# Two mixture layers behind an attention on one core: four accumulator banks by name, twelve first copies on VectorE, a last partial sum scaled early

## The chip, the core and the metric

The kernel runs on one core of a Trainium2 chip. The metric is the time of one execution on the device in microseconds (us). The core has five engines that work beside each other, each in the order of its own instructions: TensorE (PE) for matmuls, VectorE (DVE), ScalarE (ACT), GpSimd (POOL) and SyncE (SP), which here only starts transfers (DMAs). Matmuls write into PSUM, eight banks of 128 x 512 words; all else works out of SBUF. An instruction waits for those of other engines by semaphores.

## The reference

```python
def _attn_ref(q, k, v, w_pre, w_post):          # (4, 12, 448, 64)
    scores = scale * np.matmul(q, k.transpose(0, 1, 3, 2))
    scores = np.einsum('bhij,hg->bgij', scores, w_pre)
    attn = softmax(scores)
    attn = np.einsum('bhij,hg->bgij', attn, w_post)
    return np.matmul(attn, v)

def _moe_ref(x, w_in, w_out):                   # 1792 x 768, 768 x 2048, 2048 x 768
    h = x @ w_in
    g = np.where(h > 0.0, h, np.exp(np.minimum(h, 0.0)) - 1.0)
    return g @ w_out

def _moe2_ref(x, w_in, w_out, g_ln):            # 768 x 1024, 1024 x 768
    h = x @ w_in
    solu = h * softmax(h)
    ln = (solu - mu) / np.sqrt(var + 1e-06) * g_ln
    return ln @ w_out
```

The output of each is the input of the next. The weights of both layers arrive as float64 words.

## The kernel before

Attention fills the time to about 360, the first mixture layer ("first MoE") 360 to 821, the second 822 to the end. Every float32 matmul is made of three, from operands split into a high part and a remainder.

**First MoE.** The 2048 hidden features are cut into eight groups `fg` of 256, the tokens into four blocks `tb` of 448. For each (fg, tb), `hid` (line 377) makes two tiles of 128 features in 18 matmuls each; `elu` turns one into g by ACT (Relu, line 391, and Exp, line 392) and DVE (line 393), and ACT and POOL split g into `gh` and `glo` (lines 388, 389). `outp(fg, tb)` (line 872) makes six tiles `e` of 128 output features, six matmuls each (line 883), and brings every tile out of its PSUM bank into the accumulator `x1[tb]`: in group 0 by an ACT copy (line 897), later by a DVE addition (line 900). PE runs hid of one block, then outp of the block before it. The tiles of `outp` come from a pool `ps_o` of four banks under one tag; the pool decides which of the four is next. When the loop is done the pool's banks go to the second MoE.

**Filler work.** Between these steps stands work that needs no PE. Weights are loaded as 64-bit words into a ring `ws` of four buffers (SP, line 210) and decoded: DVE clamps (line 218), ACT scales (line 219), and DVE shifts, takes the sign and joins (lines 223, 227, 231). Six pieces per group are the next `fg`'s weights. After these, the second MoE's weights are made and stored to DRAM: `wi_spill` (twelve pieces) and `w2_group(k)`, k from 0 to 3. A group decodes four blocks of `w_out`, p12, p11, p22 and p21, takes differences T1, T3, T2, T4 (DVE, line 320) for a multiplication by Strassen's scheme in Winograd's form, and splits and stores seven results (ACT cast, line 333; POOL subtraction, line 334; a DMA from POOL's queue, line 341). p21's load takes the buffer of an earlier store.

The order on each engine is that of the code, and a small planner places the filler: `run` and `work` keep a modelled time of PE and of DVE, `paced(until)` issues filler steps of 0.78 us (`DVE_STEP`) as long as DVE's modelled time stays below `until`, and `tick` takes the next step whose landing time (`land`, `PD`) is over. In the last group, after outp(7, 1) has been written, `drain(True)` issues all filler steps that are left with these landing times ignored.

**Second MoE.** `hid2(t)` (line 1022) makes 14 token tiles of h, each in two PSUM banks; softmax and the normalisation's moments follow. Then seven products per pair of token tiles, P1 to P7 (line 1094), and `behind` (line 1096) adds each one to partial sums in `ob`: c11, c12 of one token tile, c21, c22 of the next. P5's bank is also added to c12 (line 1114); P3, the last product, is added to c12. What is final is multiplied by the normalisation's factor `col(9, t)` on ACT (line 1117) and goes out by DMA.

Of the kernel before, what the change touches and what calls it, by code (L numbers as in the profile page):

```python
# [9 lines left out]
F32 = mybir.dt.float32  # L10
# [3 lines left out]
AF = mybir.ActivationFunctionType  # L14
ALU = mybir.AluOpType
AX = mybir.AxisListType
PSUM = bass.MemoryType.PSUM

NB, NH, S, D = 4, 12, 448, 64
DM, F1, F2 = 768, 2048, 1024  # L20
NT = NB * S
ECH = DM // 128
# [50 lines left out]
def kernel(ctx: ExitStack, tc: tile.TileContext, qa, kt, vt, wpre, wpost,  # L73
# [4 lines left out]
    nc = tc.nc  # L78
# [3 lines left out]
    def pool(name, bufs=1, side="left", space=None):  # L82
        kw = {"space": space} if space is not None else {"side": side}
        p = tc.alloc_tile_pool(name=name, bufs=bufs, reuse_waits="tile", **kw)
        pools[name] = p
        return p
# [56 lines left out]
    pe_t, dve_t = 0.0, 0.0  # L143

    def run(us):

        nonlocal pe_t, dve_t
        dve_t = max(dve_t, pe_t)
        pe_t += us

    def work(us, ready=0.0):

        nonlocal dve_t
        dve_t = max(dve_t, ready) + us
# [86 lines left out]
    def w1_ready(fg, pieces):  # L241

        while fg and any((fg, i) not in w1_done for i in pieces):
            work(DVE_STEP)
            tick(1, force=True)
# [122 lines left out]
    def hid(fg, tb, ft, kcs=range(ECH)):  # L368
        wh, wl = w1[fg][0], w1[fg][1]
        xh, xl = xT[tb]  # L370
        if kcs[0] == 0:
            ring, p = ("sc", ps_sc) if (tb, ft) not in ((1, 1), (3, 1)) else ("h", ps_h)
            h_t[fg, tb, ft] = p.tile([128, 512], F32, tag=ring, name="h")
        ps = h_t[fg, tb, ft]
        for kc in kcs:
            for n, (a, x) in enumerate(((wh, xh), (wh, xl), (wl, xh))):
                nc.tensor.matmul(ps[:, :S], a[:, kc * FG + ft * 128:kc * FG + (ft + 1) * 128], x[:, kc, :],  # L377
                                 start=kc == 0 and n == 0, stop=kc == ECH - 1 and n == 2)
# [32 lines left out]
    def op(rank, emit, deps=(), new=(), uses=(), more=0.0, lag=None, port=False, **us):  # L411

        o = Op()
        o.port = port
        o.rank, o.emit, o.deps, o.new, o.us, o.more, o.lag = rank, emit, [d for d in deps if d is not None], new, us, more, lag
        for b in chain(new, uses):
            b.users.append(o)
        ops.append(o)
        return o
# [73 lines left out]
    t, nf, t_hid = T0, 0, None  # L493
# [36 lines left out]
    def dma(out, in_, e="sp"):  # L530
        {"act": nc.scalar, "pool": nc.gpsimd, "sp": nc.sync}[e].dma_start(out=out, in_=in_)
# [63 lines left out]
    o = op(7.0, lambda e: dma(wpre_t, wpre), sp=.5, lag=7.0)  # L595
# [37 lines left out]
    for u, sl in enumerate(units):  # L633
# [62 lines left out]
        o = op(r0 + 3.2, guard, ex, [], [sb], port=True, dve=.07)  # L696
        o = op(r0 + 3.3, inv, [o], [], [sb], dve=.07)
        ow = op(r0 + 3.4, weigh, [o, o_wpost], [wb], [sb], port=True, dve=.3, pool=.38)
        r0 = t_post[u]
        o = op(r0, post, ex + [ow], pob, eb + [wb], pe=POST)  # L700
# [5 lines left out]
    for c in range(NC):  # L706
# [12 lines left out]
        for n in range(2):  # L719
# [11 lines left out]
            o = op(r, mm, at_ops[c] + ov, [avb], [vb, at_b[c]], pe=AV * w / 120)  # L731
# [10 lines left out]
            o = op(r + AV + .2, take, [o], [xb], [avb], act=.36, dve=.42)  # L742
# [4 lines left out]
    for n in range(16):  # L747
        sl = slice((n % 8) * 192, (n % 8) * 192 + 192)
        src, dst = (wo1 if n > 7 else wi1)[0, :, sl], w1s[n // 8][:, sl]
# [38 lines left out]
        o = op(t0, load, [last], [sb], sp=.5, lag=11.0)  # L788
        o = op(t0 + 4, clamp, [o], [], [sb], dve=.17)
        oa = op(t0 + 4.5, scale, [o], [], [sb], act=.26)  # L790
        o = op(t0 + 5, loword, [o], [], [sb], dve=.17)
        o = op(t0 + 5.5, sign, [o], [], [sb], dve=.27)
        o = op(t0 + 6, join, [oa, o], [], [sb], dve=.27)
# [55 lines left out]
    for ft in range(2):  # L849
        o = None  # L850
        for p in range(3):
            o = op(t_hid + HD + ft * .01, lambda e, ft=ft, p=p: hid(0, 0, ft, range(2 * p, 2 * p + 2)),
                   need + [o] + [sc_ev[lc, h] for h in range(NH)], pe=HID / 3)
# [10 lines left out]
    x1 = [x1_p.tile([128, ECH, S], F32, tag=f"x1_{tb}", name=f"x1_{tb}", bufs=1) for tb in range(NB)]  # L864
# [3 lines left out]
    for tb in range(2, NB):  # L868
        xT_alloc(tb, pool(f"xT{tb}"))
    ps_h = pool("ps_h", 1, space=PSUM)  # L870
    ps_o = pool("ps_o", 4, space=PSUM)
    def outp(fg, tb, rest):
        w1_ready(fg, range(3, 6))
        wh, wl = w1[fg][2], w1[fg][3]
        gs = [g_t.pop((fg, tb, ft)) for ft in range(2)]
        for e in range(ECH):
            run(1.21)
            ps = ps_o.tile([128, 512], F32, tag="o", name="o")
            n = 0
            for ft in range(2):  # L880
                gh, glo = gs[ft]
                for a, x in ((wh, gh), (wl, gh), (wh, glo)):
                    nc.tensor.matmul(ps[:, :S], a[:, ft * DM + e * 128:ft * DM + (e + 1) * 128], x,  # L883
                                     start=n == 0, stop=n == 5)
                    n += 1
            if fg == 0 and tb < 2:
                if e % 2 == 0:
                    x_hi(tb + 2, e // 2)
                else:
                    x_lo(tb + 2, e // 2, nc.vector)  # L890
                    if tb == 0:
                        x_load(3, e // 2)
            else:
                paced(pe_t + DVE_LAG)
            spend(1.13)
            if fg == 0:
                nc.scalar.copy(x1[tb][:, e, :], ps[:, :S])  # L897
            else:
                work(.61, pe_t + .1)
                nc.vector.tensor_tensor(x1[tb][:, e, :], x1[tb][:, e, :], ps[:, :S], ALU.add)  # L900
            if rest:
                if len(rest) == 2:
                    work(.61)
                rest.pop(0)()
# [91 lines left out]
    def col(i, t, n=1):  # L996
        return sm[:, i, t:t + n]
# [98 lines left out]
    def behind(q, x):  # L1096


        t, n = 2 * q, 384
        ps = bank.pop(x)[:, :n]  # L1100
        if x in ("P1", "P7"):
            ob_t[t + (x == "P7")] = pools["wstg"].tile([128, 1024], F32, tag="ws", name="ob", bufs=4)
        c11, c12 = (ob_t[t][:, i * n:i * n + n] for i in range(2))
        if x == "P1":
            nc.scalar.copy(c11, ps)
            return
        if x in ("P6", "P2"):
            dst, src = (c12, c11) if x == "P6" else (c11, c11)
        else:
            c21, c22 = (ob_t[t + 1][:, i * n:i * n + n] for i in range(2))  # L1110
            dst, src = {"P7": (c21, c12), "P5": (c22, c21), "P4": (c21, c21), "P3": (c12, c12)}[x]
        nc.vector.tensor_tensor(dst, ps, src, ALU.add)
        if x == "P5":
            nc.vector.tensor_tensor(c12, ps, c12, ALU.add)
        if x not in ("P6", "P7"):
            tt, hf = {"P5": (t + 1, 1), "P2": (t, 0), "P3": (t, 1), "P4": (t + 1, 0)}[x]
            nc.scalar.activation(out=dst, in_=dst, func=AF.Copy, scale=col(9, tt))
            dma(out[tt * 128:(tt + 1) * 128, hf * n:hf * n + n], dst)

    prep = [[(l_sum, "S1"), (l_hi, "A11"), (l_sum, "S2"), (l_lo, "A11")], [(l_hi, "S2"), (l_hi, "S1"), (l_sum, "S3"), (l_lo, "S2")],  # L1120
# [6 lines left out]
    for t in range(NTT):  # L1127
        ps = hid2(t)
# [92 lines left out]
```

## Time and profile before

| | |
|---|---|
| median of three runs | 1047.11 us (1046.87 to 1049.83) |
| profiled execution | 1046.41 us |
| its span, first to last instruction | 1044.6 us |
| PE busy | 1021.1 us, 98% |
| DVE busy | 732.6 us, 70% |
| ACT busy | 556.1 us, 53% |
| POOL busy | 286.2 us, 27% |
| share of PE in the chain that ended last | 88% |

The profile follows one execution. Busy time of an engine is the sum of its instructions. "Idle before, releaser" is how long an engine stood ahead of an instruction and what ended that. The chain that ended last is followed back from the last instruction. The clock that TensorE was granted is at its full level in all forty slices of the span.

### The profile page before, as it was taken

What the parts mean: (1) busy time and instruction counts of PE and PEld (TensorE: products, weight loads), DVE (VectorE), ACT (ScalarE), POOL (GpSimd) and SP (SyncE); (2) the same over time, 40 slices, a digit from 0 to 9 for tenths busy, and PEclk for the clock granted to TensorE, in tenths of its full rate; (3) what the DMA queues carried; (4) which work ended last, traced back from release to release, by engine and by line L of the source; (5) the groups of instructions that cost most, each with busy time, mean ns of one, the idle gap of its engine ahead of it and who ended that gap; (6) DMA issues with size and microseconds to landing.
All of it is one profiled execution on the core that took longest, in us unless ns stands there. A gap on an engine that the chain in (4) does not pass through costs nothing.

```text
span 1044.6 us, 28451 instructions
## 1 busy us (share of the span) xinstructions
PE 1021.1 (98%) x11604; PEld 859.6 (82%) x11604; DVE 732.6 (70%) x1371; ACT 556.1 (53%) x1178; POOL 286.2 (27%) x297
## 2 busy tenths in 40 slices
PE   6899999999999999999999999999999999999998
PEld 2467777777666898999999999999999888889998
DVE  5687787677677357689978687786855355668874
ACT  3476677777677575544444345444444245555543
POOL 5011011111013524556534445444544200000000
PEclk9999999999999999999999999999999999999999
DMA  6776876776856542653523232423282533838741
GB/s 199 219 229 187 242 214 211 222 227 188 237 157 185 156 143 92 206 177 132 182 77 115 96 106 83 149 87 126 81 297 106 200 107 106 187 106 202 151 102 61
DMA packets 142442, 165.79 MB, mean 159 GB/s; under 512 B 79496, under 2 KB 119272, under 8 KB 142312
## 3 DMA queue, kind: packets, MB, share of 16 engines
q1 hardware_dynamic: 136207, 143.27, 46.2%
q0 software_dynamic: 3968, 17.30, 4.3%
q10 hardware_dynamic: 2137, 3.41, 1.1%
q8 instruction: 91, 1.49, 0.6%
q14 instruction: 39, 0.32, 0.1%
HBM read 88.02 MB, written 37.22 MB: 120 GB/s over the span
## 4 chain that ended last, share of the span: by engine, by line
PE 88%; DMA 3%; DVE 3%; ACT 3%; issue 2%; POOL 1%; SPq 0%; ACTq 0%; DVEq 0%; POOLq 0%
PE h L377 21%; PE o L883 21%; PE h L1022 11%; PE w L1094 10%; PE av L728 7%; PE po L679 7%; PE pm L646 6%; PE sc L574 6%; DMA sp<-sev 2%; ACT e L656 1%; DMA q<-in_qa_dram 1%; DVE st L651 1%; DVE wy L231 1%; ACT at L687 0%; DVE wq L227 0%
## 5 line engine op out<-in xcount | busy, mean ns | idle before, releaser
L656 ACT ACTIVATE e<-pm,st 128x448 f32<-128x448 f32 x180 | 113.7, 636 | 63.0 <-DVE st L651 54.7
L651 DVE TENSOR_REDUCE st<-pm 128x1 f32<-128x448 f32 x180 | 105.7, 617 | 54.6 <-PE pm L646 52.8
L883 PE MATMUL o<-gh,woh 128*128 128x448 f32 x384 | 140.6, 366 | 1.0 <-ACT x L897 0.8
L883 PE MATMUL o<-glo,woh 128*128 128x448 f32 x384 | 140.1, 365 | 0.0
L883 PE MATMUL o<-gh,wol 128*128 128x448 f32 x384 | 139.6, 363 | 0.0
L679 PEld LDWEIGHTS po<-wr,e 60*64 60x64 f32 x5040 | 101.0, 134 | 37.5 <-issue 23.8
L574 PE MATMUL sc<-kt,q 64*64 64x448 f32 x816 | 119.0, 559 | 9.2 <-DMA kt<-in_kt_dram 4.2
L900 DVE TENSOR_TENSOR x<-x,o 128x448 f32<-128x448 f32 x168 | 101.7, 613 | 28.7 <-PE o L883 27.7
L389 POOL TENSOR_TENSOR glo<-g,gh 128x448 fp32r<-128x448 f32 x64 | 83.3, 1301 | 124.6 <-ACT gh L388 122.2
L667 POOL TENSOR_TENSOR wr<-wpost_t,st 128x120 f32<-128x120 f32 x90 | 35.8, 398 | 281.8 <-DVE st L663 226.5
L646 PE MATMUL pm<-sp,wpre_t 64*64 64x448 f32 x720 | 108.6, 555 | 3.8 <-ACT e L656 2.3
L679 PE MATMUL po<-wr,e 60*64 60x60 f32 x5040 | 107.4, 219 | 3.4 <-issue 2.8
L377 PE MATMUL h<-xh,wih 128*128 128x448 f32 x288 | 105.4, 366 | 0.0
L377 PE MATMUL h<-xh,wil 128*128 128x448 f32 x288 | 105.1, 365 | 0.0
L377 PE MATMUL h<-xl,wih 128*128 128x448 f32 x288 | 104.7, 363 | 0.0
L1022 PE MATMUL h<-wi,x2h 128*128 128x512 f32 x308 | 98.7, 395 | 0.8 <-issue 0.8
L728 PEld LDWEIGHTS av<-at,v 128*64 128x64 f32 x1632 | 75.4, 137 | 15.0 <-issue 4.6
L393 DVE SCALAR_TENSOR_TENSOR g<-g,h 128x448 f32<-128x448 f32 x64 | 39.5, 616 | 66.0 <-ACT g L392 65.5
L728 PE MATMUL av<-at,v 128*64 128x120 f32 (+5 forms) x1632 | 82.6, 258 | 0.7 <-ACT x L735 0.5
L883 PEld LDWEIGHTS o<-gh,woh 128*128 128x128 f32 x384 | 72.1, 188 | 7.3 <-ACT x L897 1.4
L883 PEld LDWEIGHTS o<-glo,woh 128*128 128x128 f32 x384 | 72.0, 188 | 6.0
L883 PEld LDWEIGHTS o<-gh,wol 128*128 128x128 f32 x384 | 72.1, 188 | 5.6
(124 smaller groups left out, 1988.0 us busy)
## 6 DMA issues: line engine op xcount, KB each, us to landing
sp<-sev SPq DMA_DIRECT2D x93, 210.0 KB
ws<-in_wi_dram SPq DMA_DIRECT2D x33, 512.0 KB
ws<-in_wo_dram SPq DMA_DIRECT2D x21, 512.0 KB
lts<-sq SPq DMA_DIRECT2D x14, 512.0 KB
lt<-lts SPq DMA_DIRECT2D x56, 128.0 KB
q<-in_qa_dram SPq DMA_DIRECT2D x34, 192.0 KB
v<-in_vt_dram SPq DMA_DIRECT2D x24, 256.0 KB
wis<-ws POOLq DMA_DIRECT2D x12, 512.0 KB, 3.2
```

The lines of the kernel that those rows point to most:

```text
L377: nc.tensor.matmul(ps[:, :S], a[:, kc * FG + ft * 128:kc * FG + (ft + 1) * 128], x[:, kc, :], start=kc == 0 and n == 0, stop=kc == ECH - 1 ...
L389: nc.gpsimd.tensor_tensor(glo, g, f(gh), ALU.subtract)
L574: nc.tensor.matmul(T[key][i][64 * x:64 * x + 64, :S], q[sl, h % 6 // 2, 64 * x:64 * x + 64], k[sl, :], start=True, stop=True)
L646: nc.tensor.matmul(ps_t[u][r][64 * s:64 * s + 64, :S], wpre_t[p, :], sp_t[c][p, g, :], start=True, stop=True)
L651: nc.vector.tensor_reduce(out=st_t[u][:P, r:r + 1], in_=ps_t[u][r][:P, :S], op=ALU.max, axis=AX.X, negate=True)
L656: nc.scalar.activation(out=t[:P], in_=ps_t[u][r][:P, :S], func=AF.Exp, bias=st[:P, r:r + 1], scale=1.0, accum_out=st[:P, 2 + r:3 + r])
L679: nc.tensor.matmul(out[:, :, 5 * r:5 * r + 5], e_t[u, r][sl, 64 * n:64 * n + 64], wr_t[u][sl, r].rearrange("p (g a) -> p g a", a=5), start ...
L728: nc.tensor.matmul(ps[64 * k:64 * k + 64, i, :], v_t[CH[c][0]][:, 6 * n + 2 * i + k, q, :], at_t[c][:, q, 6 * n + 2 * i + k, :w], start=q ...
L883: nc.tensor.matmul(ps[:, :S], a[:, ft * DM + e * 128:ft * DM + (e + 1) * 128], x, start=n == 0, stop=n == 5)
L900: nc.vector.tensor_tensor(x1[tb][:, e, :], x1[tb][:, e, :], ps[:, :S], ALU.add)
L1022: nc.tensor.matmul(ps[:, hf * 512:hf * 512 + 512], a[:, k, :], w, start=n == 0, stop=n == 3 * ECH - 1)
L1094: nc.tensor.matmul(ps[:, :384], a[:, s, k, :], w, start=k == 0 and i == 0, stop=k == 3 and i == 2)
```

## The change

Three edits. The four banks of `outp` get one tag each, and the tile (tb, e) takes number (6 tb + e) mod 4. In group 0 the accumulators of token blocks 2 and 3 are filled by DVE copies instead of ACT copies, and each books 0.55 us of DVE with the planner. In `behind`, c12 is multiplied by `col(9, t)` on ACT behind P5's addition, and P3's bank is multiplied by it and added to c12 by one DVE instruction (`scalar_tensor_tensor`), without the scaling on ACT after it.

```diff
-    ps_o = pool("ps_o", 4, space=PSUM)
+    ps_o = pool("ps_o", 1, space=PSUM)
@@ outp
-            ps = ps_o.tile([128, 512], F32, tag="o", name="o")
+            ps = ps_o.tile([128, 512], F32, tag=f"o{(tb * ECH + e) % 4}", name="o")
...
-            if fg == 0:
+            if fg == 0 and tb < 2:
                 nc.scalar.copy(x1[tb][:, e, :], ps[:, :S])
+            elif fg == 0:
+                work(.55, pe_t + .1)
+                nc.vector.tensor_copy(x1[tb][:, e, :], ps[:, :S])
             else:
                 work(.61, pe_t + .1)
                 nc.vector.tensor_tensor(x1[tb][:, e, :], x1[tb][:, e, :], ps[:, :S], ALU.add)
@@ behind
-        nc.vector.tensor_tensor(dst, ps, src, ALU.add)
+        if x == "P3":
+            nc.vector.scalar_tensor_tensor(dst, ps, col(9, t), src, ALU.mult, ALU.add)
+        else:
+            nc.vector.tensor_tensor(dst, ps, src, ALU.add)
         if x == "P5":
             nc.vector.tensor_tensor(c12, ps, c12, ALU.add)
+            nc.scalar.activation(out=c12, in_=c12, func=AF.Copy, scale=col(9, t))
         if x not in ("P6", "P7"):
             tt, hf = {"P5": (t + 1, 1), "P2": (t, 0), "P3": (t, 1), "P4": (t + 1, 0)}[x]
-            nc.scalar.activation(out=dst, in_=dst, func=AF.Copy, scale=col(9, tt))
+            if x != "P3":
+                nc.scalar.activation(out=dst, in_=dst, func=AF.Copy, scale=col(9, tt))
             dma(out[tt * 128:(tt + 1) * 128, hf * n:hf * n + n], dst)
```

The order of instructions on the engines, as the built programs have it, moves at three places. The line numbers after the change are three higher behind line 900. First, VectorE in group 0 while outp(0, 2) runs; before, only filler and g stand there:

```order
L231 SCALAR_TENSOR_TENSOR wy<-wy,wq 128x512
L218 TENSOR_SCALAR ws<-ws 128x512
L393 SCALAR_TENSOR_TENSOR g<-g,h 128x448
L223 TENSOR_SCALAR wq<-ws 128x512
L227 SCALAR_TENSOR_TENSOR wq<-ws,wq 128x512
```

The same place of VectorE after the change, where x_2 is the accumulator of token block 2:

```order
L227 SCALAR_TENSOR_TENSOR wq<-ws,wq 128x512
L900 COPY x_2_6992<-o 128x448
L231 SCALAR_TENSOR_TENSOR wy<-wy,wq 128x512
L900 COPY x_2_6992<-o 128x448
L393 SCALAR_TENSOR_TENSOR g<-g,h 128x448
L900 COPY x_2_6992<-o 128x448
L218 TENSOR_SCALAR ws<-ws 128x512
L900 COPY x_2_6992<-o 128x448
```

Each copy stands alone among filler steps, at most one or two of them between two copies, and the filler steps that stood there come later. Second, VectorE at the end of the first MoE, from the last additions of outp(7, 1), into x_1, to the first of outp(7, 2), into x_2; before:

```order
L900 TENSOR_TENSOR x_1_6991<-x_1_6991,o 128x448
L227 SCALAR_TENSOR_TENSOR wq<-ws,wq 128x384
L900 TENSOR_TENSOR x_1_6991<-x_1_6991,o 128x448
L231 SCALAR_TENSOR_TENSOR wg<-wg,wq 128x384
L320 TENSOR_TENSOR wg<-wg 128x384
L393 SCALAR_TENSOR_TENSOR g<-g,h 128x448
L900 TENSOR_TENSOR x_2_6992<-x_2_6992,o 128x448 x2
```

And after, on VectorE from outp(7, 1)'s third addition on:

```order
L320 TENSOR_TENSOR wg<-wg 128x384
L903 TENSOR_TENSOR x_1_6991<-x_1_6991,o 128x448 x3
L218 TENSOR_SCALAR ws<-ws 128x384
L223 TENSOR_SCALAR wq<-ws 128x384
L227 SCALAR_TENSOR_TENSOR wq<-ws,wq 128x384
L231 SCALAR_TENSOR_TENSOR wg<-wg,wq 128x384
L320 TENSOR_TENSOR wg<-wg 128x384 x2
L218 TENSOR_SCALAR ws<-ws 128x384
L223 TENSOR_SCALAR wq<-ws 128x384
L227 SCALAR_TENSOR_TENSOR wq<-ws,wq 128x384
L231 SCALAR_TENSOR_TENSOR wg<-wg,wq 128x384
L320 TENSOR_TENSOR wg<-wg 128x384
```

p22's and p21's decode and three subtractions (T3 and T2 as "x2", T4 as the last row) stand between the additions of outp(7, 1) and the g of the next block, which follows this piece. Third, the last rows of ScalarE; before:

```order
L1105 COPY ob<-w 128x384
L1117 ACTIVATE ob<-ob,sm 128x384 x4
```

And after, where line 1121 is the new scaling of c12:

```order
L1108 COPY ob<-w 128x384
L1121 ACTIVATE ob<-ob,sm 128x384
L1125 ACTIVATE ob<-ob,sm 128x384 x3
```

The scaling that stood last has moved ahead of three others.

## Rows read from the trace of the kernel before

**Rows 1.** PE's two longest waits from 360 to 822: total us, times, longest
```profile
PE o L883 <- ACT x L897: 0.8, 1, 0.8
PE h L1022 <- issue: 0.8, 1, 0.8
```

**Rows 2.** Chain that ended last, two pieces: start, us, what
```profile
799.04 7.30 PE h L377 x36
806.34 14.59 PE o L883 x72
```

**Rows 3.** Timeline of ACT, 414 to 419: start, us, instruction, [idle before <-releaser]
```profile
417.11 0.66 ACT L219 ACTIVATE wy<-ws 128x512 f32<-128x512 f32 x1 [0.77 <-POOL ws L287]
417.68 0.95 ACT L897 COPY x<-o 128x448 f32<-128x448 f32 x2
```

**Rows 4.** Groups by line and form: count | busy us, mean ns | idle before
```profile
L580 DVE COPY sev<-sc 128x448 f32<-128x448 f32 x87 | 52.6, 615 | 11.4 <-PE sc L574 11.1
L393 DVE SCALAR_TENSOR_TENSOR g<-g,h 128x448 f32<-128x448 f32 x64 | 39.5, 616 | 66.0 <-ACT g L392 65.5 <-POOL wil L255 0.5
```

**Rows 5.** Timeline at the border of the two MoEs, 820 to 823
```profile
820.97 0.62 DVE L900 TENSOR_TENSOR x<-x,o 128x448 f32<-128x448 f32 x1 [0.60 <-PE o L883]
...
821.69 0.47 PE L1022 MATMUL h<-wi,x2h 128*128 128x512 f32 x1 [0.76 <-issue]
```

**Rows 6.** Last pieces of the chain that ended last
```profile
1040.51 0.57 DVE ob L1112
...
1041.10 0.61 ACT ob L1117
```

**Rows 7.** Timeline of ACT: a scaling of the last pair
```profile
1034.86 0.62 ACT L1117 ACTIVATE ob<-ob,sm 128x384 f32<-128x384 f32 x1 [6.35 <-DVE ob L1112]
```

**Rows 8.** Timeline of DVE, 784 to 807, decode steps and g
```profile
785.02 0.35 DVE L218 TENSOR_SCALAR ws<-ws 128x384 f32<-128x384 f32 x1
785.29 0.36 DVE L223 TENSOR_SCALAR wq<-ws 128x384 int32<-128x384 int32 x1
...
786.34 0.56 DVE L231 SCALAR_TENSOR_TENSOR wg<-wg,wq 128x384 int32<-128x384 int32 x1
...
797.45 1.78 DVE L223 TENSOR_SCALAR wq<-ws 128x384 int32<-128x384 int32 x1
...
800.69 0.54 DVE L231 SCALAR_TENSOR_TENSOR wg<-wg,wq 128x384 int32<-128x384 int32 x1
803.56 0.56 DVE L320 TENSOR_TENSOR wg<-wg 128x384 f32<-128x384 f32 x1 [2.33 <-POOL ws L334]
805.75 0.62 DVE L393 SCALAR_TENSOR_TENSOR g<-g,h 128x448 f32<-128x448 f32 x1 [1.63 <-ACT g L392]
```

**Rows 9.** Timeline of POOL, 783 to 814
```profile
784.33 0.56 POOL L341 DMA_DIRECT2D w2s13T<-ws  x1 [0.41 <-POOL ws L334]
...
797.84 1.16 POOL L389 TENSOR_TENSOR glo<-g,gh 128x448 fp32r<-128x448 f32 x1
802.51 1.02 POOL L334 TENSOR_TENSOR ws<-wg,ws 128x384 fp32r<-128x384 f32 x1 [3.50 <-ACT ws L333]
...
807.06 1.15 POOL L389 TENSOR_TENSOR glo<-g,gh 128x448 fp32r<-128x448 f32 x1 [0.33 <-ACT gh L388]
...
811.75 1.85 POOL L1010 TENSOR_TENSOR x2l<-x,x2h 128x768 fp32r<-128x768 f32 x1
```

**Rows 10.** Line 210 (weight loads), 780 to 800: ns min/median/max, first and last start
```profile
L210 SPq DMA_DIRECT2D ws<-in_wo_dram x1: 332/332/332, 787.9 to 787.9; - x1
```

**Rows 11.** Two stretches: busy of PE, PEld, DVE, ACT, POOL, PE's clock, DMA share, GB/s
```profile
790.00:790.50 0.50, 0.50 (x4) 0.47 (x3) 0.00 (x1) 0.46 (x1) 0.00 (x0) 1.00 0.73 279
790.50:791.00 0.50, 0.50 (x5) 0.46 (x4) 0.00 (x0) 0.50 (x3) 0.31 (x1) 1.00 0.01 0
```

**Rows 12.** DMA issues, 760 to 830: count, size, median us to landing
```profile
w2s13T<-ws POOLq DMA_DIRECT2D x4, 384.0 KB, 2.6
w2s12T<-ws POOLq DMA_DIRECT2D x1, 384.0 KB, 7.1
```

## The prediction, as it was made

> **What bounds the kernel now.** I read the share of busy time first: TensorE (PE) works 98% of a span of 1044.6 us, and in the forty slices of the page its granted clock stands at full speed throughout. So an edit can win only a gap in PE, a piece ahead of its first or behind its last matmul, and it can lose only by making a new gap. The second view is the list of PE's waits from 360 to 822, the first MoE with its two ends: its two longest gaps in 462 us are 0.8 us each, one behind an accumulator copy of line 897 and one, put down to "issue", at the first matmul of the second MoE [rows 1]. From 450 to 806 there is none. The third is the chain of work that ended last: in it outp(7,2) and outp(7,3) are one piece of 72 matmuls from 806.34 to 820.93 without a gap, behind hid(7,3,·) from 799.04 [rows 2], and after PE's last product two instructions follow, one on VectorE (DVE) and one on ScalarE (ACT) [rows 6]. So there are three places where this change can gain, 0.8, 0.76 and some 0.6 us, and every other effect has to be looked for as a new wait.
>
> The profiled execution took 1046.41 with a span of 1044.6; the three timed runs have the median 1047.11, 0.70 above it. I make the sum against 1044.6 and add 2.5 (1047.11 − 1044.6) for the median. A measurement of this kernel can tell about 0.3%, here 3.1 us, from no change.
>
> **Copies on DVE in feature group 0.** Removed: 12 ACT copies, two of them in token block 2 at 417.68, where ACT was late: it waited 0.77 for GpSimd (POOL), then ran a scaling of 0.66 that stands ahead of the copies [rows 3]; the bank came free late and PE stood 0.8 [rows 1]. With a copy on DVE that bank no longer hangs on ACT. Added: 12 DVE copies of 128x448 out of PSUM. DVE has such copies in the attention, at 0.615 us [rows 4]: 12 × 0.615 = 7.4 us of DVE. They cost PE nothing where each comes less than three tiles late: a tile is 14.59/12 = 1.216 us of PE [rows 2], and four banks leave 3 × 1.216 = 3.65 us between the end of a tile and the next use of its bank. On DVE only one or two filler steps of some 0.55 us stand between two copies in the order of the changed program; cover is 3.65, need 1.2 to 1.7. If a filler ahead of a copy waited for ACT longer than 2 us, the price would be the same kind of gap as the one removed. I take **−0.8**, with 0 as the other end.
>
> **The named turn.** In the program of before the banks come in the turn 4, 7, 6, 5, and the last tile of the first MoE sits in bank 5. The first tile of the second MoE takes banks 4 and 5. Now the turn is 4, 5, 6, 7, and the last two tiles sit in 6 and 7. In the trace the last accumulation starts at 820.97 and takes 0.62, to 821.59, and the first matmul of line 1022 starts at 821.69 after 0.76 of idle [rows 5]. The profile calls this "issue", but 0.10 behind the end of an addition in the same bank is what a wait for the bank looks like. Its other input, the low half x2l, is not it: POOL began it at 811.75 and took 1.85 [rows 9]. I take **−0.76**; the other end is 0, if the gap is PE's own.
>
> **The last partial sum.** Before, the end is P3's addition on DVE (0.57 at 1040.51), then the scaling on ACT (0.61 at 1041.10), then the output's DMA [rows 6]. Now c12 is scaled by ACT after P5, and P3's DVE instruction multiplies its bank and adds. The fused instruction costs what the addition costs: at 384 columns a fused integer one takes 0.56 [rows 8] against 0.57, and at 448 columns with an operand in PSUM 0.616 beside 0.615 of a copy [rows 4]. So the end loses ACT's 0.61 and the 0.02 ahead of it: **−0.63**. The added ACT scaling per pair of token tiles takes 0.62; the last one falls near 1035, where ACT stood idle for 6.35 before its instruction [rows 7], some 4 us before P3 needs it. It costs 0.
>
> **What booked time does to the filler queue.** Each of the 12 copies also books 0.55 us with the planner (`work(.55)`), so `paced` finds less room and spends fewer filler steps in group 0. Nothing is lost there, but the queue of decode steps shifts later, and at its end stands `drain(True)` after outp(7,1), which puts all that is left in one row, without pause for a landing. Before, that was six steps: of DVE's, only T4's subtraction stood ahead of g(7,3,0). After, it is 22: p22's decode, T3's and T2's subtractions, p21's load and decode, T4's subtraction, with their ACT casts, POOL subtractions and stores. All stand on DVE ahead of g(7,3,0) and of outp(7,2)'s accumulations, and PE needs the latter: tile 4 of outp(7,2) takes tile 0's bank, at 806.34 + 4 × 1.216 = 811.20.
>
> When does DVE get there? p21's load goes into the buffer that T1's store empties. T1's subtraction now follows the third addition of outp(7,1); that tile ends at 799.04 − 3 × 1.216 = 795.39 [rows 2], so the subtraction runs from about 795.95 to 796.5. With a cast on ACT (0.6), 1.02 of subtraction on POOL and the 0.41 between that and a store [rows 9], the store is issued at about 798.6. Before, the same store was issued at 784.33 [rows 9] and the load behind it at 787.9 [rows 10]: 3.57. The load's bytes were through at 790.5, since the DMA share falls from 0.73 to 0.01 there [rows 11]: 2.6 more. So p21 is there at 798.6 + 3.57 + 2.6 = 804.8. Its decode took p22's, of the same shape, 1.88 before (785.02 to 786.34 + 0.56), and joins at 806.7. A decode can be slower: its shift took 0.36 at 785.29 but 1.78 at 797.45, while POOL ran line 389 from 797.84 (1.16) [rows 8, 9]. POOL is busy here with T3's and T2's subtraction and store, so the other end is 1.4 to 1.6 more: 808.3. From the join on I use the row of before: join end 801.23 (800.69 + 0.54), T4's subtraction 803.56, g at 805.75 [rows 8]. T4's subtraction waits for POOL's of B21, which began 1.28 behind the join (802.51) or now begins when POOL is through with B22, T3 and T2. p22's decode starts behind the last addition of outp(7,1), at 799.6, and joins at 801.5; B22's subtraction ends 1.28 + 1.02 later, at 803.8; then come three stores (0.41 + 0.56 each) and two subtractions, 2.9 + 2.0: 808.7. So B21's begins between 808.7 and 808.3 + 1.28 = 809.6, ends 1.02 later, and g(7,3,0) starts 2.2 behind T4's (805.75 − 803.56): **812.0 to 812.8**, instead of 805.75.
>
> Tile 0's accumulation ends 1.15 behind that start (0.53 between two issues, 0.62), at 813.2 to 814.0, so PE, due at 811.20, stands 2.0 to 2.8. The two tiles left and outp(7,3) follow as before; g(7,3,1) comes two additions behind g(7,3,0), and its low half is used only by the last matmul of each tile. The loss is 2.0 to 2.8; I take the middle, **+2.4**, as neither row for the shift is nearer. Below, it ends at 0 if p21's load lands 2.5 earlier and POOL with it.
>
> The shift of 1.78 is also where a rule can be weighed. It began 0.39 ahead of POOL's instruction, and POOL's then took 1.16, as much as the undisturbed one at 807.06, 1.15 [rows 8, 9]. The Trainium skill (SBUF — State Buffer, "Who interferes with whom") says that the shared port goes, for the whole instruction, to whichever of VectorE and GpSimd issues first, and that the other blocks. By that the shift, being first, should have kept 0.36 and POOL's should have grown; the row shows the reverse. By the Trainium skill's rule the drain's shift would cost little when first, and the loss would be its lower end, 2.0; the row speaks against it.
>
> **Sum.** −0.80 − 0.76 − 0.63 + 2.4 = +0.2: span 1044.8, median **1047.3**. That is no change.
>
> **The rivals.** *Drain hidden.* If stores land and POOL goes faster than before's rows, g(7,3,0) starts by 810.0, tile 0 is empty by 811.2 and nothing is lost: 1047.1 − 2.2 = 1044.9. For it: POOL's waits in the drain overlap in part. Against: it needs 2 us less in a chain whose every link has a row. Chance 0.14.
>
> *Late load (slower than before).* The store ahead of p21's load landed in 2.6 at the median, but one of the same shape took 7.1 [rows 12]. That is 4.5 more: p21 at 809.3, join at 811.2, POOL 812.5 to 813.5, T4, g at 815.7, and PE stands 5.7. Net +3.5: 1050.6. It decides from a landing some 4 us late (loss over 5.3). For it: p12's and p11's loads now stand behind eleven wi loads on SP, which also fills the DMA engines. Against: the 7.1 was at 765, while those loads ran; by 799 they are done. Chance 0.11.
>
> *The turn does nothing.* The gap at 821 is PE's own and stays: 1047.3 + 0.76 = 1048.1. For it: the profile's word "issue". Against: 0.10 behind the addition, in the same bank. Chance 0.12.
>
> *A copy stuck in group 0.* DVE, in order, waits with a filler for ACT ahead of a copy, and the 0.8 comes back or doubles: 1048.1 to 1048.9. Chance 0.06.
>
> **Chances.** Forecast 0.55, drain hidden 0.14, turn idle 0.12, late load 0.11, copies stuck 0.06, else 0.02. Faster by over 0.3% needs more than all three gains: 0.03. Slower by over 0.3% is the late load and half of what a longer chain in the drain may bring: 0.14. Within 0.3%: 0.83. The range takes in the drain hidden below (1044.8), and above the bounds of the drain with an idle turn and part of the late load: 1049.6.
>
> **What would show it.** Right: PE's waits lose the 0.8 at line 897 and the gap at the border; a wait of 2 to 3 us appears in outp(7,2) near 811, released by line 903 on DVE; ahead of it a row of decode steps on DVE and g near 812; the chain ends on DVE's fused instruction. Wrong: no wait in outp(7,2) (drain hidden), one over 5 us (late load), waits near 410 to 430 on DVE copies, or a gap of 0.76 still at the border.

## The result: 0.9% slower, and where the time is

The changed kernel takes 1058.36 us in the median of 11 runs (1052.22 to 1062.45); beside them the kernel before takes 1048.74 (11 runs, 1045.92 to 1051.66). The ratio is 1.0086, with a 95% interval of 1.0063 to 1.0109: slower by some 9 us, where no change (1047.3, at most 1049.6) was forecast. The profiled execution has a span of 1057.0, against 1044.6.

The spans of both kernels can be cut at the same places: the start of the first block of full hid work behind the attention, the start of each outp, the first matmul of the second MoE, the end. Each figure is the start of a matmul of PE in the trace (a few records are missing, so 0.1 to 0.2 is not to be read into them).

| stretch | before | after | difference |
|---|---|---|---|
| attention, up to hid(0,1) | 360.09 | 362.60 | +2.5 |
| first MoE, up to the end of outp(0,3) | 59.47 | 58.35 | −1.1 |
| hid(1,1) to outp(3,3) | 175.43 | 182.37 | +6.9 |
| hid(4,1) up to outp(7,2) | 211.18 | 211.32 | +0.1 |
| outp(7,2) and outp(7,3), up to the second MoE | 15.52 | 19.87 | +4.4 |
| second MoE and end | 222.91 | 222.49 | −0.4 |

The attention is the same code. Its end lies anywhere from 358.4 to 363.5 in the 13 profiles of this study, in kernels that differ only behind it, so its +2.5 is spread between executions and no part of the change. What is left is +9.9, close to the 9.6 between the medians.

PE's waits of the kernel after, from 360 to 840 (total us, times, longest; compare [rows 1]):

```profile
PE o L883 <- DVE x L903: 8.4, 6, 3.4
```

Both gaps of before are gone, the one at line 897 and the one at the border. In their place PE waits six times for a DVE addition, 8.4 us in all; one of these waits is the forecast one in outp(7,2), the other five, all in groups 1 and 2 and 4.9 together, were not forecast. Each of the longer ones makes its block longer by some 0.25 more than the wait itself (outp(1,0): 2.23, and 2.50 longer), and outp(1,2) and outp(2,2), whose gaps of 0.1 are too short for the list, lose 0.4 each: so 4.9 become the 6.9 of the table. The first and the last wait in PE's timeline:

```profile
435.51 0.47 PE L883 MATMUL o<-gh,woh 128*128 128x448 f32 x1 [2.23 <-DVE x L903]
...
823.11 0.74 PE L883 MATMUL o<-gh,woh 128*128 128x448 f32 x1 [3.44 <-DVE x L903]
```

**The first wait, 435.51.** DVE's timeline ahead of it:

```profile
427.20 0.62 DVE L393 SCALAR_TENSOR_TENSOR g<-g,h 128x448 f32<-128x448 f32 x1 [1.50 <-ACT g L392]
427.74 0.68 DVE L227 SCALAR_TENSOR_TENSOR wq<-ws,wq 128x512 int32<-128x512 int32 x1
428.53 1.69 DVE L231 SCALAR_TENSOR_TENSOR wy<-wy,wq 128x512 int32<-128x512 int32 x1
432.32 1.53 DVE L218 TENSOR_SCALAR ws<-ws 128x512 f32<-128x512 f32 x1 [2.11 <-DMA ws<-in_wi_dram]
433.78 0.42 DVE L223 TENSOR_SCALAR wq<-ws 128x512 int32<-128x512 int32 x1
434.23 0.69 DVE L227 SCALAR_TENSOR_TENSOR wq<-ws,wq 128x512 int32<-128x512 int32 x1
434.84 0.61 DVE L903 TENSOR_TENSOR x<-x,o 128x448 f32<-128x448 f32 x1
```

Here outp(1,0) began at 428.25, so its tile 0 was complete at 429.5. Its addition stands behind five decode steps. The clamp (line 218) of a weight piece stands there before its load has landed and holds the engine for 2.11; the clamp then runs 1.53, where it takes 0.4 undisturbed. The addition comes at 434.84, 5.4 us behind the tile; it takes 0.61 itself, and the bank's cover is 3.65. In the kernel before the same addition stands behind the same five steps, but the load had landed. There outp(1,0) began at 426.86, its tile 0 was complete at 428.08, and the addition came 0.8 behind it:

```profile
424.59 0.62 DVE L393 SCALAR_TENSOR_TENSOR g<-g,h 128x448 f32<-128x448 f32 x1 [5.04 <-ACT g L392]
...
425.92 1.68 DVE L231 SCALAR_TENSOR_TENSOR wy<-wy,wq 128x512 int32<-128x512 int32 x1
427.53 0.42 DVE L218 TENSOR_SCALAR ws<-ws 128x512 f32<-128x512 f32 x1
...
428.92 0.62 DVE L900 TENSOR_TENSOR x<-x,o 128x448 f32<-128x448 f32 x1
```

The join ran long in both kernels, 1.68 and 1.69 where it takes 0.7 undisturbed, so it is not what differs. Of the 4.5 by which the addition now comes later behind its tile, 2.1 are the wait for the load, 1.1 the long clamp, and 1.2 a later start of the whole row: g, which stands ahead of the five steps, started 2.27 ahead of outp(1,0) before and 1.05 ahead of it now.

**The last wait, 823.11**, is the forced drain. DVE's timeline from the last addition of outp(7,1) on (compare [rows 8]):

```profile
807.54 0.62 DVE L903 TENSOR_TENSOR x<-x,o 128x448 f32<-128x448 f32 x1 [0.60 <-PE o L883]
...
813.26 1.25 DVE L218 TENSOR_SCALAR ws<-ws 128x384 f32<-128x384 f32 x1 [0.41 <-DMA ws<-in_wo_dram]
814.43 0.35 DVE L223 TENSOR_SCALAR wq<-ws 128x384 int32<-128x384 int32 x1
814.81 1.91 DVE L227 SCALAR_TENSOR_TENSOR wq<-ws,wq 128x384 int32<-128x384 int32 x1
816.83 0.56 DVE L231 SCALAR_TENSOR_TENSOR wg<-wg,wq 128x384 int32<-128x384 int32 x1
819.71 0.56 DVE L320 TENSOR_TENSOR wg<-wg 128x384 f32<-128x384 f32 x1 [2.33 <-POOL ws L334]
821.90 0.62 DVE L393 SCALAR_TENSOR_TENSOR g<-g,h 128x448 f32<-128x448 f32 x1 [1.63 <-ACT g L392]
822.44 1.14 DVE L903 TENSOR_TENSOR x<-x,o 128x448 f32<-128x448 f32 x2
```

And the wait costs more than its 3.44. Stretches around it (from:to, length, busy time of PE with its matmuls, of PE's weight loads, DVE, ACT, POOL, then PE's granted clock, DMA share, GB/s):

```profile
822.00:823.00 1.00, 0.00 (x0) 0.00 (x0) 1.00 (x3) 0.45 (x1) 0.56 (x1) 0.91 0.15 55
823.00:824.00 1.00, 0.89 (x2) 0.83 (x3) 0.58 (x2) 0.97 (x3) 0.79 (x1) 0.50 0.65 258
824.00:825.00 1.00, 1.00 (x4) 0.89 (x3) 0.80 (x2) 0.31 (x2) 0.35 (x1) 0.50 0.35 135
825.00:826.00 1.00, 1.00 (x4) 0.87 (x4) 1.00 (x3) 1.00 (x2) 0.50 (x1) 0.50 0.00 0
826.00:827.00 1.00, 1.00 (x6) 0.91 (x5) 0.41 (x1) 0.89 (x2) 1.00 (x2) 0.89 0.00 0
827.00:828.00 1.00, 1.00 (x7) 0.91 (x6) 0.62 (x1) 0.00 (x0) 1.00 (x1) 1.00 0.05 16
```

The granted clock falls to 0.50, the 1.2 GHz level, at the end of the idle stretch and stays there for 3.4 us, from 822.8 to 826.2: matmuls start 0.37 apart instead of 0.20. So outp(7,2) and outp(7,3), 14.59 without a wait, take 19.87, 5.3 more. In a second profile of this kernel (below) the same wait of 3.44 stood at full clock, and they took 18.46: 3.9 go with the wait and 1.4 with the slow clock.

The end of the chain that ended last has become what was forecast, DVE's fused instruction and nothing on ACT behind it (compare [rows 6]):

```profile
1053.44 0.62 DVE ob L1116
```

### The profile page after: what moved, and what is told of

It reads as the page before. It is cut to its first block, busy times and chain, and to the rows that moved or that the text cites. A ratio compares the mean times of both kernels' runs of the same rounds, so it can differ in the third digit from the quotient of the medians.

```text
span 1057.0 us, 28454 instructions
## 1 busy us (share of the span) xinstructions
PE 1025.6 (97%) x11604; PEld 861.6 (82%) x11604; DVE 741.0 (70%) x1383; ACT 552.9 (52%) x1166; POOL 282.9 (27%) x297
## 4 chain that ended last, share of the span: by engine, by line
PE 75%; DMA 7%; DVE 7%; issue 5%; ACT 2%; POOL 2%; SPq 0%; ACTq 0%; POOLq 0%; DVEq 0%
PE h L377 15%; PE o L883 14%; PE h L1025 11%; PE w L1097 10%; PE po L679 7%; PE av L728 7%; PE pm L646 6%; PE sc L574 6%; DMA sp<-sev 2%; DMA ws<-in_wo_dram 1%; DVE wq L227 1%; DMA v<-in_vt_dram 1%; DVE ws L218 1%; DVE wq L223 1%; DVE wy L231 1%
```

## The experiments

The theory after the result: the loss comes from the order of the filler alone. The booked 0.55 us per copy shifts the decode steps, so that in groups 1 and 2 steps that wait or run long stand ahead of additions, and that the drain is long. The rivals: VectorE's own new load of 7.4 us; the named turn; one late transfer in one execution.

The table has the stretches of every profile, as differences from the profile before, in us (waits and slow clock together). The fourth column is the tail, outp(7,2) to the second MoE.

| kernel | up to outp(0,3) | to outp(3,3) | tail | second MoE, end | ratio of runs, 95% interval |
|---|---|---|---|---|---|
| after | −1.1 | +6.9 | +4.4 | −0.4 | 1.0086 [1.0063, 1.0109] |
| after_again | −1.1 | +7.9 | +2.9 | −0.4 | 1.0091 [1.0058, 1.0124] |
| book_only | −1.2 | +6.1 | +6.6 | +0.2 | 1.0085 [1.0057, 1.0113] |
| all_unbooked | +1.1 | +0.5 | −0.9 | −0.5 | 0.9995 [0.9975, 1.0014] |
| turn_end | 0.0 | −0.4 | −0.9 | −0.4 | 0.9964 [0.9944, 0.9984] |
| turn_end_2 | 0.0 | 0.0 | −0.9 | −0.5 | 1.0000 [0.9981, 1.0020] |
| turn_end_relu | +0.1 | +0.5 | −0.9 | −0.6 | 0.9996 [0.9978, 1.0013] |
| relu_first | −0.7 | +4.8 | +5.4 | −0.4 | 1.0091 [1.0064, 1.0118] |
| late_drain | −1.1 | +6.5 | −0.7 | +5.3 | 1.0077 [1.0050, 1.0104] |
| drain_busy | −1.1 | +6.2 | +3.0 | −0.4 | 1.0094 [1.0063, 1.0126] |
| book_block2 | −0.5 | +5.1 | −0.9 | −0.6 | 1.0028 [1.0012, 1.0043] |
| copies_block2 | −0.6 | +1.6 | −0.9 | −0.6 | 1.0034 [1.0014, 1.0054] |

### The booking alone

On the kernel before:

```diff
             if fg == 0:
+                if tb >= 2:
+                    work(.55, pe_t + .1)
                 nc.scalar.copy(x1[tb][:, e, :], ps[:, :S])
```

> The kernel before with one edit: in group 0 the accumulators of token blocks 2 and 3 stay ACT copies, but each still books 0.55 us of VectorE with the planner. So the filler queue stands as in the changed kernel, and none of its copies, bank turn or last sum. Theory of the shifted queue: the loss is in the order alone, so PE waits for VectorE's additions in groups 1 and 2 (4 to 5 us in all) and near the forced drain (3 to 4 us, with a lower granted clock behind it) stand here too: 8 to 12 us over before, some 1056 to 1060. Rival, VectorE's own load (12 copies, 7.4 us): without the copies no such wait, within 1 us of before; the drain alone may leave 3 to 5.

Measured 1057.88 against 1048.29. PE's waits from 355 to 840:

```profile
PE o L883 <- DVE x L902: 7.6, 6, 3.4
PE h L1024 <- issue: 0.8, 1, 0.8
```

The whole loss is here, in a kernel in which no instruction was added to DVE: only the planner's account of time was changed. The border's 0.8 is still there, since the turn is the old one. And the gap at line 897 is gone although the copies are ACT's: with the shifted filler ACT's copies came in time. So the 0.8 that the changed kernel wins there is also the work of the order, not of the other engine.

### Everything but the booking

The changed kernel without one line:

```diff
             elif fg == 0:
-                work(.55, pe_t + .1)
                 nc.vector.tensor_copy(x1[tb][:, e, :], ps[:, :S])
```

> The changed kernel without the line that books 0.55 us for each copy: copies on VectorE, the named turn and the last sum stay, the filler queue stands as before. Theory of the shifted queue: no wait of PE for additions in groups 1 and 2, no wait in outp(7,2); of the gains stay -0.8 (line 897), -0.76 (border) and -0.6 (end): 1.5 to 2.5 us under before. Rival, VectorE's own load: waits of PE behind additions or copies between 400 and 510, time at or above that of before, by up to 5 us.

Measured 1048.68 against 1048.29, ratio 0.9995. PE's waits from 355 to 840:

```profile
PE o L883 <- DVE x L899: 1.8, 2, 1.1
PE o L883 <- DVE x L902: 0.6, 1, 0.6
```

Neither side has it all. The tail's wait and those of groups 1 and 2 are gone, as the shifted queue wants it, but for the 0.6 in outp(1,1), a block that lost 0.4 in the kernel before too. But with the old order DVE's copies are late in group 0, twice, 1.8 us together, and this takes back what border and end give. The time was to be 1.5 to 2.5 under before; it is not to be told from it.

### The turn and the last sum alone

> The kernel before with the named turn and the last sum scaled in advance, and the ACT copies as they were. Both theories: the gap of 0.8 at line 897 stays, that of 0.76 at the border of the two layers goes, the end behind PE's last product is 0.5 to 0.6 shorter: 1.3 us under before, hardly to be told from it by time, so the profile decides. If the border's gap is PE's own and not a wait for the bank, it stays at 0.7 to 0.8.

Measured 1045.2 against 1048.29, ratio 0.9964. The waits from 355 to 840 keep line 897 and lose the border:

```profile
PE o L883 <- ACT x L897: 0.9, 1, 0.9
```

The stretch from outp(7,2) to the second MoE is 14.60 in place of 15.52, and behind it 222.48 in place of 222.91. That is 1.35 us that the edits give; the runs showed 3. So the same kernel was run again:

> The named turn and the last sum on the kernel before, once more. Its stages behind the attention add up to 1.4 us under before in the profile (0.9 at the border, 0.4 at the end), while its timed runs were 3 us under. Theory: the 1.4 is what the edits give and the rest is the spread of the attention's end from run to run (358 to 363 in the profiles), so about 1 to 2 us under before here, its interval overlapping 1. Rival: the 3 us come back.

Measured 1046.14 against 1046.9, ratio 1.0000 (0.9981 to 1.0020). The stages again give 1.5, the runs nothing that can be told. The first interval did not reach 1 and the second has its middle on it: behind the attention the stages of the two profiles agree within 0.4 us, the medians against before only within some 3.

### The changed kernel again

> The changed kernel once more, to see which of its waits come back. Theory of the shifted queue: again waits of PE for additions between 430 and 510 and one of 3 to 4 us in outp(7,2), with half the clock for some us behind it; the waits between 430 and 510 hang on when loads land, so their sizes may differ by 1 or 2 us each. Time 8 to 12 over before. Rival, a late single transfer in the profiled execution: the waits are elsewhere or gone, and the time is nearer to before's.

Measured 1059.58 against 1048.29. The waits return in the same turns of groups 1 and 2 (sum 4.8 beside 4.9) and in outp(7,2) (3.4). So they hang on the order, not on one transfer. What differs is the clock: in this execution it fell behind the first wait, in outp(1,0), which was 2.23 as in the profile above where it had not fallen, and it did not fall behind the one in outp(7,2), whose stretches were:

```profile
816.00:818.00 2.00, 0.40 (x2) 0.02 (x1) 0.56 (x1) 0.95 (x2) 1.33 (x3) 1.00 0.07 28
818.00:820.00 2.00, 0.16 (x1) 0.17 (x2) 1.37 (x3) 1.29 (x3) 1.24 (x3) 1.00 0.43 169
820.00:822.00 2.00, 2.00 (x11) 1.85 (x12) 1.38 (x3) 1.28 (x3) 1.09 (x1) 1.00 0.50 197
```

### No forced drain

The changed kernel with `drain(True)` moved behind the last outp:

```diff
-            if tb == 2 and fg + 1 == NFG:
-                drain(True)
     outp(*prev, [])
-    drain()
+    drain(True)
```

> The changed kernel with one edit: nothing is forced after outp(7,1); the filler left then is paced through the last token block, and what is left after outp(7,3) is issued there. Theory: VectorE gets to outp(7,2)'s additions in time, so the wait of 3.4 us near 820 and the half clock behind it (1.7 us) go, while the waits between 430 and 550 stay: 5 us under the changed kernel, some 1053 to 1054. Rival, the tail's loss comes from the later filler itself, wherever it stands: the wait only moves, by 1 us or so, to the border of the layers or into the second layer's first tiles.

Measured 1055.76 against 1047.27. The tail's wait went (14.79, no gap in outp(7,2)), and a new one came at the second matmul of the second MoE, from 800 to 850 the only one:

```profile
PE h L1023 <- POOL x2l L1011: 2.7, 1, 2.7
```

POOL's timeline says why:

```profile
827.68 1.01 POOL L334 TENSOR_TENSOR ws<-wg,ws 128x384 fp32r<-128x384 f32 x1 [1.18 <-ACT ws L333]
829.09 0.56 POOL L341 DMA_DIRECT2D w2s13T<-ws  x1 [0.41 <-POOL ws L334]
829.67 3.58 POOL L1011 TENSOR_TENSOR x2l<-x,x2h 128x768 fp32r<-128x768 f32 x2
```

The low halves that the second MoE's first two tiles need now stand behind the last filler on POOL. Before, they were made at 811.75 [rows 9] and 813.55. Again the clock fell to 0.50, from 831 to 837, and the second MoE is 5.7 longer than in the changed kernel. The rival was right for both places tried: late filler costs at the tail, because one engine or the other has it ahead of something that PE waits for.

### TensorE kept busy in the wait

The changed kernel with 16 unused matmuls ahead of tile 4 of outp(7,2):

```diff
+            if (fg, tb, e) == (NFG - 1, 2, 4):
+                spare = ps_sc.tile([128, 512], F32, tag="sc", name="spare")
+                for i in range(16):
+                    nc.tensor.matmul(spare[:, :S], wh[:, :128], gs[0][0], start=i == 0, stop=i == 15)
```

> The changed kernel with 16 matmuls into a spare bank (3.2 us of TensorE at full clock) ahead of tile 4 of outp(7,2), where TensorE waited 3.4 us. They add work that nothing uses. Theory that the lower clock behind that wait follows from the idle time before it: the granted clock stays at 1.00 from 818 to 830, and the stretch from the start of outp(7,2) to the second layer's first matmul is 1.7 us shorter although TensorE does more. Rival, the clock falls for another reason, such as the load on POOL and VectorE there: it falls to 0.50 as before, and nothing is won.

Measured 1056.31 against 1047.27. The clock stayed full, and PE still waits 0.22 behind the spare matmuls:

```profile
816.00:818.00 2.00, 2.00 (x12) 1.85 (x11) 0.56 (x1) 0.98 (x3) 1.33 (x3) 1.00 0.10 40
818.00:820.00 2.00, 1.78 (x9) 1.33 (x8) 1.42 (x3) 1.31 (x3) 1.26 (x3) 1.00 0.40 157
820.00:822.00 2.00, 2.00 (x11) 1.85 (x11) 1.37 (x4) 1.28 (x3) 1.05 (x1) 1.00 0.50 197
```

The tail takes 18.49 in place of 19.87, 1.4 less, though PE does more; the ratio of its four runs, 1.0094, does not show that gain. POOL and DVE were as busy as before, so in this execution their load alone did not lower the clock. But the changed kernel's second profile had 18.46 with the idle wait and no fall. With PE idle the clock fell behind this wait in three profiles of four (after, book_only, relu_first), with PE busy in none of one: that agrees with idle time as the cause, and one profile is too little to call it shown.

### The Relu first

The changed kernel with the first ACT instruction of `elu` ahead of its turn's filler:

```diff
+                rest = elu(fg, tb, ft)
                 if early:
                     tick(TI - ft, more=False)
                 else:
                     paced(pe_t + 1.0)
                 spend(3.4)
-                rest = elu(fg, tb, ft)
```

> The changed kernel with one edit: the first ACT instruction of elu (Relu) is issued ahead of the filler of that turn instead of behind it; VectorE's order is the same. In the changed kernel a scaling of line 219 that waits for VectorE's clamp stands ahead of the Relu in some turns (472.66 behind 3.5 us of waiting, hidden tile ready at 472.1), so g and all VectorE work behind it come about 1 us late. Theory: this is part of the waits between 430 and 550, which shrink from about 5 us by 2 to 3, time 2 to 3 us under the changed kernel. Rival, these waits come only from loads that land late and from decode steps stretched beside POOL: they stay within 1 us.

ACT in the changed kernel, where the hidden tile was ready at 472.1:

```profile
472.66 0.69 ACT L219 ACTIVATE wy<-ws 128x512 f32<-128x512 f32 x1 [3.50 <-issue]
473.25 0.52 ACT L391 ACTIVATE g<-h 128x448 f32<-128x448 f32 x1
```

Measured 1056.14 against 1047.27. Groups 1 and 2 lose 4.8, where the five other profiles with all twelve bookings lose 6.1 to 7.9. The same turns show in each of these: outp(2,3) loses 0.8 to 1.1 and here 0.2, outp(1,3) 0.8 to 1.0 and here 0.3, outp(2,0) 1.7 and here 1.15; the first, outp(1,0), loses 2.0, within the 1.3 to 3.6 of the others. So by this one profile the late Relu is a part, some 1.9 us, just under the 2 to 3 of the theory; the medians cannot tell it. On the kernel with the turn and the last sum alone the same edit brings nothing:

> The named turn and the last sum scaled in advance on the kernel before, ACT copies kept, with the Relu ahead of the filler of its turn as well. Theory: with the order of before there is no wait between 430 and 820 to shrink, so it is within 1 us of the turn and the last sum alone: 1 to 3 us under before, and the gap of 0.8 at line 897 may go or stay, since the copies stand at the same place.

Measured 1046.77 against 1047.27, and the gap at line 897 stays at 0.8.

### Half of the bookings

The named turn, the last sum, ACT copies, and 0.55 booked in token block 2 alone; the drain is as short as before:

```diff
             if fg == 0:
+                if tb in (2,):
+                    work(0.55, pe_t + .1)
                 nc.scalar.copy(x1[tb][:, e, :], ps[:, :S])
```

> The named turn and the last sum scaled in advance, ACT copies throughout, and 0.55 us booked for each of the six copies of token block 2 alone. In the built order the forced drain is as short as before and groups 1 to 3 stand nearly as before. Theory, the loss comes from where the shifted queue puts its steps and not from booked time as such: the gap at line 897 goes (booking alone removed it with 12 bookings), groups 1 to 3 and the tail stay within 0.5 us of before, so 2 to 2.5 us under before. Rival, any booked time in group 0 brings the waits of groups 1 to 3: half of their 6 us, 1 to 2 us over before.

Measured 1049.09 against 1046.9, ratio 1.0028 (1.0012 to 1.0043). The tail is the short one, but groups 1 and 2 lose 5.1. The rival comes nearer than the theory, but not by half of the same waits: there is one of 0.79 in outp(1,0), and a new one of 2.46 in outp(1,1) with a slow clock behind it. There the clamp of another piece waits 2.00 for its load, and g, the two long steps and the addition all come late behind it. DVE and PE around it:

```profile
443.95 0.43 DVE L218 TENSOR_SCALAR ws<-ws 128x512 f32<-128x512 f32 x1 [2.00 <-DMA ws<-in_wi_dram]
...
447.55 1.81 DVE L227 SCALAR_TENSOR_TENSOR wq<-ws,wq 128x512 int32<-128x512 int32 x1
449.40 1.53 DVE L231 SCALAR_TENSOR_TENSOR wy<-wy,wq 128x512 int32<-128x512 int32 x1
...
452.24 0.61 DVE L902 TENSOR_TENSOR x<-x,o 128x448 f32<-128x448 f32 x1
```

```profile
452.91 0.74 PE L883 MATMUL o<-gh,woh 128*128 128x448 f32 x1 [2.46 <-DVE x L902]
```

The second kernel with half of the bookings has DVE copies in block 2, booked, and the rest as in the changed kernel:

```diff
-            if fg == 0 and tb < 2:
+            if fg == 0 and tb != 2:
                 nc.scalar.copy(x1[tb][:, e, :], ps[:, :S])
```

> The changed kernel with the copies of token block 3 back on ACT and not booked; those of block 2 are DVE copies, booked. Theory: as with the booking of block 2 alone, the gap at line 897 goes, no wait in groups 1 to 3 over 0.5 us, a short drain: 2 to 2.5 us under before. Rival, VectorE's copies are late behind stretched decode steps, as where they were not booked (1.1 us more in group 0): 0 to 1 us under before.

Measured 1050.27 against 1046.9, ratio 1.0034. The profile has only 1.6 lost in groups 1 and 2 and no late copy on DVE (one on ACT in outp(0,3) costs 0.4), and its stages behind the attention add up to 0.3 under before; the medians say slower, and what made the other runs so is not shown. Neither half is worth having.

## Why the prediction was wrong, point by point

**The copies on DVE (−0.8): the size came, the reason was wrong.** The gap went, and the first stretch is 1.1 shorter. But booking alone removed it with ACT copies, and DVE copies without booking made it larger (+1.1). The 0.615 per copy was right (12 copies, 0.612 in the mean). The prediction also put the gap into token block 2; by the sequence of matmuls it stands in outp(0,3), block 3.

**The named turn (−0.76): right.** The stretch to the second MoE is 0.9 shorter in every kernel with the turn and a short drain, and "issue" was the wait for the bank. The rival that the turn does nothing falls.

**The last partial sum (−0.63): right, with 0.4 to 0.6 by the stages.** The fused instruction took 0.62 at the end where the addition had taken 0.57, so the end itself is 0.58 shorter.

**The filler queue: here the forecast failed.** The step was "Nothing is lost there, but the queue of decode steps shifts later": I followed the shift to its far end and took what lies between as harmless, because PE waits nowhere from 450 to 806 in the trace of before. That absence was a property of the old order. In the new one, groups 1 and 2 lost 6.9, two thirds of the whole, for a term of 0. The trace of before held the warning: the shift of 1.78 at 797.45 [rows 8], and the cover of 3.65 that I had worked out, against five decode steps ahead of tile 0's addition. Long steps alone did not break the old order. Ahead of outp(2,1)'s first addition three of the five ran long, and it came 2.85 behind its tile; with its own 0.61 that is inside the cover:

```profile
499.15 1.67 DVE L231 SCALAR_TENSOR_TENSOR wy<-wy,wq 128x512 int32<-128x512 int32 x1
500.74 1.38 DVE L218 TENSOR_SCALAR ws<-ws 128x512 f32<-128x512 f32 x1
502.04 1.52 DVE L223 TENSOR_SCALAR wq<-ws 128x512 int32<-128x512 int32 x1
...
504.21 0.61 DVE L900 TENSOR_TENSOR x<-x,o 128x448 f32<-128x448 f32 x1
```

In the new order the sums go over it. By the blocks of the changed kernel's first profile, outp(1,0) and outp(2,0), where a landing of 2.1 and 0.8 stands in the row, lose 4.2. Outp(1,3) and outp(2,3), with three long steps and g some 1 us late, lose 1.6, and outp(1,1), outp(1,2) and outp(2,2), with two or three long steps, 1.2. The rival "a copy stuck in group 0" was this mechanism, but I asked it only of the twelve new copies, at 0.06 and 0.8 to 1.6 us, and not of the 168 additions behind the shifted steps.

**The drain (+2.4): the chain was right, the price half of it, 5.3 measured.** p21's load was through at 5.9 behind the end of outp(7,1) (807.35 to 813.26), 5.8 by the forecast. Its decode joined at 817.39, 4.1 later, and not 1.9 to 3.5: two steps ran long, clamp 1.25 and sign 1.91, where I had allowed one. The wait was 3.44 for 2.0 to 2.8. And the slow clock behind it, 1.4 here, was no term of the sum at all, since no row of before showed a wait long enough. The reading that the clock was full throughout was also too coarse: a slice of the page is 26 us long and its 9 stands for 90% or more, and in the attention of before the trace has the clock at 0.50 from 14.8 to 18.2, behind waits of PE of 1.03 and 0.80.

In the long step the weighed rule can be read again. POOL's timeline beside it:

```profile
811.25 1.00 POOL L334 TENSOR_TENSOR ws<-wg,ws 128x384 fp32r<-128x384 f32 x1 [3.32 <-DVE wg L320]
...
815.27 1.03 POOL L334 TENSOR_TENSOR ws<-wg,ws 128x384 fp32r<-128x384 f32 x1
```

The sign step began at 814.81, 0.46 ahead of POOL's subtraction; it took 1.91, and POOL's 1.03, as undisturbed. By the Trainium skill (SBUF — State Buffer, "Who interferes with whom") the one that issues first keeps the shared port and the other blocks. As in the row of before, the one that began first by the trace was stretched, so the rule could not price it.

**The rivals.** "Drain hidden" and "late load" did not occur: the load landed when the chain said.

**What stays open.** It is open how the 6.9 divides between steps that wait for a load, long steps, and the late Relu. The trace divides it by block, as above, and outp(1,0)'s row by its parts; of the three causes only the Relu was tried by a run, with some 1.9. No run took a landing or a long step away without moving the order.

## What to carry to other kernels

Where a planner's account of time decides the order, a number booked is an edit of the whole order behind it: compare the built orders over their full length, and at each changed place ask what stands ahead of an instruction that PE waits for, whether it can wait for a transfer there, and what it takes at its longest and not in the mean. That an order has no waits is no margin; the margin is the cover (here 3.65 us) less the addition itself and the longest sum that can stand ahead of it, counted from the latest start of that row. When edits are bundled, price and try each alone: here two gave 1.4 us by the stages and the third, a planner's account of 0.55 us that changed no instruction, cost some 9.6.

## What was not expected of the hardware

TensorE's granted clock fell to 0.50, the 1.2 GHz level, behind single idle waits of 2.23 us (after_again), 2.46 (book_block2), 2.67 (late_drain) and 3.44 (after, book_only, relu_first). It stayed there for 3.4 us, and for 6.8 in late_drain, book_only and relu_first. Beside the same wait at full clock that cost 1.6 behind the 2.23 and 1.4 behind the 3.44, and 2.4 to 2.7 behind the 3.44 where it lasted 6.8. A wait of the same 2.23 (after, 435.51) and one of 3.44 (after_again) left it at 1.00. So a gap's length alone did not tell whether its price would grow by half or more.
